# First block of an attention and feed-forward kernel: o in products of 512 tokens, three zero products fewer, and a new order of squares and first weight

## The chip, the cores and the metric

The kernel runs on one core of a Trainium2 chip. The metric is the device time of one execution in microseconds (us). Five runs of the kernel before are known; lower is better. TensorE is called PE here (its weight loads PEld), VectorE DVE, ScalarE ACT, GpSimd POOL, SyncE SP.

## The reference

Two parts follow each other. The first is linear attention over 8 batches, 8 heads, 576 tokens and a head size of 64; the second is a feed-forward layer with a leaky ReLU over 4608 tokens, 512 model columns and 2048 hidden ones.

```python
kv = np.einsum('bhsd,bhse->bhde', k, v)
out = np.einsum('bhsd,bhde->bhse', q, kv)
rms = np.sqrt(np.mean(out * out, axis=-1, keepdims=True) + 1e-06)
attn = (out / rms * g_norm).astype(np.float32)
x = attn.transpose(0, 2, 1, 3).reshape(B * S, H * D)
h = x @ w_in
g = np.maximum(0.01 * h, h)
out = (g @ w_out).astype(np.float32)
```

The two weights arrive as 64-bit floats and are rounded on the chip to 32 bits; all products are of 32-bit floats.

## The kernel before, in words

The tokens are worked off in nine blocks of 512. The blocks after the first save products with Strassen sums; they fill most of the time and are not touched. The change lies in `first_attention`, which makes the first 512 tokens' x before the first block's products can begin, and in `round_f64`, which rounds one weight.

`first_attention` does this. PE warms up on zeros (`keep_warm`, tile `idle_ps`), turns the four q tiles of the first batch (`q_ps`, `rest_ps`; ACT and DVE copy them to `qT`) with one zero product of 256 columns behind each of the first three tiles, makes kv (`kv_ps`, two lots of 36 products, one more zero product between them) and DVE copies it (`copy_kv`). Then come the products of o, 32 of 256 tokens each: tokens 0 to 255 first (`half` 0), then the others, each with the two halves `e` of the head's columns. A product of 32-bit floats shows as two passes in the trace, so 32 products are 64 matmul records and 64 weight loads. The products use different parts of PE's array (64 rows by 32 columns), so that several run at once.

From o the root mean square comes in small steps. ACT squares (`square`), PE adds the squares up per head (`add_up`, tile `sum_ps`), ACT takes the root (`root`, tile `flat`), PE turns it (`turn`), DVE inverts it (`invert`, tile `roots`), PE spreads it (`spread`, tile `inv_ps`), and DVE multiplies x by it (`scale`). x itself is o times the gain `g_sb` (`keep`: DVE for half 0, ACT for half 1).

In between stands the rounding of the first weight (`w0 = rounding(0)`), a generator that `next` moves by a step: ACT's add and cut, then four DVE operations (lines 246, 250, 252, 255). Weights 1 to 4 are rounded behind it (`round_w`), the others within the first block. The products then use the weights in this order, one weight per eight passes of 512 columns: `h_ps` with weight 0, `h_ps` with weight 1, `o_acc` with weight 2, and so on.

Nearly all these instructions are pinned, that is, each engine runs them in the order in which the program lists them. Weight loads are issued by SP in a fixed order, each as soon as its home has been read.

Of the kernel before, what the change touches and what calls it, by code (L numbers as in the profile page):

```python
# [9 lines left out]
F32 = mybir.dt.float32  # L10
U32 = mybir.dt.uint32
I64 = mybir.dt.int64
AF = mybir.ActivationFunctionType
AX = mybir.AxisListType
ALU = mybir.AluOpType
# [8 lines left out]
def kernel(  # L24
# [36 lines left out]
    nc = tc.nc  # L61
    B, H, S, D = q.shape
    DM, DF = w_in.shape
    P = 128
    NE = DM // P
    E = 32
    NP = H // 2
    J = S // 64
    T = S // 32
    NT = 4 * P  # L70
    NB = B * S // NT
    N2 = NT // 2
# [15 lines left out]
    ps_m = ctx.enter_context(tc.tile_pool(name="ps_m", bufs=1, space=bass.MemoryType.PSUM))  # L88
# [28 lines left out]
    def matmul(*args, **kw):  # L117
        pin(nc.tensor.matmul(*args, **kw))  # L118
# [86 lines left out]
    def spare(n, name, dtype=F32):  # L205

        return gpool.tile([P, n], dtype, tag=next(spare_homes), name=name)
# [21 lines left out]
    def round_f64(dst, raw):  # L229

        a, n = dst.shape[1:]
        lo, hi = raw[:, :, 0], raw[:, :, 1]  # L240
        add = spare(a * n, "add", U32)
        pin(nc.scalar.activation(add, lo, func=AF.Copy, scale=2.0 ** -29))
        cut = spare(a * n, "cut")
        pin(nc.scalar.activation(cut, hi.bitcast(F32), func=AF.Copy, scale=2.0 ** -112))
        yield
        pin(nc.vector.tensor_scalar(cut, cut, HIGH_MOST, -HIGH_MOST, op0=ALU.min, op1=ALU.max))
        yield
        dst = dst.bitcast(U32)
        add, cut = (t.rearrange("p (a n) -> p a n", a=a) for t in (add, cut.bitcast(U32)))
        pin(nc.vector.tensor_scalar(dst, cut, 3, None, op0=ALU.logical_shift_left))  # L250
        yield
        pin(nc.vector.scalar_tensor_tensor(dst, in0=cut, scalar=0x80000000, in1=dst,
                                           op0=ALU.bitwise_and, op1=ALU.bitwise_or))
        yield
        pin(nc.vector.tensor_tensor(dst, dst, add, op=ALU.add))  # L255
# [21 lines left out]
    def rounding(j):  # L277
        if w_in.dtype == I64:
            yield from round_f64(w_jobs[j][0], w_raws.pop(j))
# [53 lines left out]
    def o_products(b, lo, hi, e, o_ps):  # L333
        for p in range(NP):
            for l in range(2):
                r = slice(64 * l, 64 * l + 64)
                matmul(o_ps[half_of(p, l)][E * p:E * p + E, :],
                       lhsT=kvs[b % 2][r, p, E * e:E * e + E],
                       rhs=qTs[b][r, p, lo - b * S:hi - b * S], start=True, stop=True)
# [124 lines left out]
    def first_attention():  # L464


        idle = ps_m.tile([P, NT], F32, tag="hd", name="idle_ps")

        def keep_warm(n=NT):
            matmul(idle[:, :n], lhsT=zeros[:, :P], rhs=zeros[:, :n], start=True, stop=True)  # L470

        keep_warm()
        keep_warm()
        qT = qTs[0] = work.tile([P, NP, S], F32, tag="qT", name="qT")
        kv_ps = kv_tiles()


        rest = ps_m.tile([64, NP, P], F32, tag="oc", name="rest_ps")
        for j in range(1, 3):
            load_w(j)  # L480

        def move(p, l, to, of):

            c = 64 * half_of(p, l)
            eng = (nc.scalar.copy, nc.vector.tensor_copy)[l]
            eng(qT[c:c + 64, p, :].rearrange("p (t j) -> p j t", j=J)[:, to, :],
                of[:, :, 64 * l:64 * l + 64])

        for p in range(NP):
            q_in = q_ins.pop((0, p))  # L490
            banks = [ps_m.tile([64, 4, P], F32, tag=t, name="q_ps")
                     for t in (("ha", "hb"), ("hc", "oa"))[p % 2]]
            for j in range(J):
                to = banks[j // 4][:, j % 4, :] if j < 8 else rest[:, p, :]
                pin(nc.tensor.transpose(to, q_in[:, j, :], ident))
            if p + 1 < NP:
                keep_warm(N2)
            for i in range(2):
                for l in range(2):
                    move(p, l, slice(4 * i, 4 * i + 4), banks[i])  # L500
        for p in range(NP):
            for l in range(2):
                move(p, l, slice(8, 9), rest[:, p:p + 1, :])
        for m in range(2):
            if m:
                keep_warm()
            attention_kv(0, m, kv_ps)
        for j in range(3, 7):
            load_w(j)
        w0 = rounding(0)  # L510
        next(w0, None)
        copy_kv(0, kv_ps)
        next(w0, None)


        x = block(0)

        o_ps = [[ps_m.tile([P, 2, N2], F32, tag=t, name="o_ps") for t in tags]
                for tags in (("hb", "hd"), ("oa", "oc"))]
        squares = [[spare(NT, "sq").rearrange("p (e n) -> p e n", e=2) for _ in range(2)]  # L520
                   for _ in range(2)]
        roots = [work.tile([P, 2, 2, NP], F32, tag="rms", name="roots", bufs=2) for _ in range(2)]
        flat = [work.tile([64, N2], F32, tag="t2k", name="flat", bufs=3) for _ in range(2)]
        sum_ps = [ps_att.tile([P, NT], F32, tag="att", name="sum_ps") for _ in range(2)]
        inv_ps = [ps_m.tile([P, 2, N2], F32, tag=t, name="inv_ps") for t in ("ha", "hc")]
        for half in range(2):
            for e in range(2):
                o_products(0, half * N2, half * N2 + N2, e,
                           [o_ps[half][l][:, e, :] for l in range(2)])

        def square(half, l):
            pin(nc.scalar.activation(squares[half][l], o_ps[half][l], func=AF.Square))

        def keep(half, l):
            for e in range(2):
                to, o = x[:, 2 * l + e, half * N2:half * N2 + N2], o_ps[half][l][:, e, :]
                if half == 0:
                    pin(nc.vector.tensor_scalar(to, o, g_sb[:, e:e + 1], None, op0=ALU.mult))
                else:
                    pin(nc.scalar.activation(to, o, func=AF.Copy, scale=g_sb[:, e:e + 1]))  # L540

        def add_up(half, l):

            for e in range(2):
                matmul(sum_ps[half][E * l:E * l + E, :N2], lhsT=group,
                       rhs=squares[half][l][:, e, :], start=(e == 0), stop=(e == 1))

        def root(half):

            pin(nc.scalar.activation(flat[half], sum_ps[half][:64, :N2], func=AF.Sqrt,  # L550
                                     scale=1.0 / D, bias=eps_sb[:64]))

        def turn(half):
            for t in range(2):
                matmul(turned(half)[:, t, :, :], lhsT=flat[half][:, t * P:t * P + P],
                       rhs=ident[:64, :64].rearrange("p (l i) -> p l i", l=2)[:, :, :NP],
                       start=True, stop=True)

        def turned(half):
            return sum_ps[half][:, N2:N2 + 4 * NP].rearrange("p (t l a) -> p t l a", t=2, l=2)  # L560

        def invert(half):
            pin(nc.vector.reciprocal(roots[half], turned(half)))

        def spread(half):

            for l in range(2):
                for t in range(2):
                    for p in range(NP):
                        matmul(inv_ps[half][E * p:E * p + E, l, t * P:t * P + P],  # L570
                               lhsT=roots[half][:, t, l, p:p + 1].to_broadcast([P, E]),
                               rhs=ident, start=True, stop=True)

        def scale(half, l):
            to = x[:, 2 * l:2 * l + 2, half * N2:half * N2 + N2]
            pin(nc.vector.tensor_tensor(
                to, to, inv_ps[half][:, l, :].unsqueeze(1).to_broadcast([P, 2, N2]), op=ALU.mult))

        for l in range(2):
            square(0, l)  # L580
            keep(0, l)
            add_up(0, l)
        next(w0, None)
        square(1, 0)
        add_up(1, 0)
        root(0)
        turn(0)
        next(w0, None)
        invert(0)
        for _ in w0:  # L590
            pass
        square(1, 1)
        add_up(1, 1)
        spread(0)
        root(1)
        turn(1)
        keep(1, 0)
        keep(1, 1)
        scale(0, 0)
        scale(0, 1)  # L600
        invert(1)
        spread(1)
        for l in range(2):
            scale(1, l)
        for j in range(1, 5):
            round_w(j)

# [503 lines left out]
```

## Time and profile before

| what | us |
|---|---|
| median of 5 runs | 929.01 |
| lowest and highest run | 926.81, 929.87 |
| the profiled execution's own time | 928.43 |
| its span, first to last instruction | 926.6 |
| PE busy in the span | 916.2 |
| first `o_ps` matmul | 14.68 |
| first `h_ps` matmul (weight 0) | 28.42 |
| `h_ps` with weight 1 | 32.31 |

The profiled execution lasts 1.83 us longer than its span, and 0.58 us less than the median. A row of the chain of waits gives its start, its length and the work; a row of the timeline gives start, busy time, engine, line, operation and count. "issue" is time for which the profile shows nothing to wait for. In the table of stretches the columns are the stretch, its length, each engine's busy time with the number of instructions, PE's granted clock (1.00 is full), the share of DMA time and GB/s.

### The profile page before, as it was taken

Reading aid. Unit: us, or ns where it says so; the run is one execution under the profiler, and the core shown is the slowest. Engines: PE = TensorE matmul, PEld = TensorE weight load, DVE = VectorE, ACT = ScalarE, POOL = GpSimd, SP = SyncE. Lnnn points to the kernel's source line nnn. Section 1 sums busy time; section 2 is a strip of 40 time slices with the busy share of each in tenths; the row PEclk is TensorE's granted clock in tenths of the full one; section 3 lists DMA queues with packets and bytes.
Section 4 is the critical chain, followed back from the end, with each engine's and each line's share of the span. In section 5 each row is a group of like instructions: output and inputs, shape, how many; then the busy total and the mean of one; then the engine's idle time right before and its main releaser. Section 6 shows DMA issues by size and latency. Waiting matters only on the chain.

```text
span 926.6 us, 17568 instructions
## 1 busy us (share of the span) xinstructions
PE 916.2 (99%) x6856; PEld 776.8 (84%) x6856; DVE 615.9 (66%) x999; ACT 328.9 (35%) x651; POOL 317.5 (34%) x318
## 2 busy tenths in 40 slices
PE   7999999999999999999999999999999999999998
PEld 4544447888998999899999999999989999999997
DVE  4866895587456876587756875687558754654454
ACT  4643632242136232433243423342343333223330
POOL 2000354967722442226211712272225322532222
PEclk9999999999999999999999999999999999999999
DMA  8999916895498679856995589758655676667642
GB/s 251 206 245 242 262 66 202 287 300 166 137 342 268 186 213 308 261 183 181 272 302 180 177 266 284 231 174 247 241 169 182 196 219 185 185 197 220 186 123 91
DMA packets 90081, 200.02 MB, mean 216 GB/s; under 512 B 9872, under 2 KB 42128, under 8 KB 90000
## 3 DMA queue, kind: packets, MB, share of 16 engines
q1 hardware_dynamic: 79536, 186.98, 68.5%
q10 hardware_dynamic: 10016, 10.75, 3.4%
q8 instruction: 54, 0.88, 0.4%
q0 software_dynamic: 448, 1.18, 0.3%
q14 instruction: 27, 0.22, 0.1%
HBM read 172.39 MB, written 26.48 MB: 215 GB/s over the span
## 4 chain that ended last, share of the span: by engine, by line
PE 96%; DVE 2%; DMA 1%; ACT 1%; issue 1%; POOL 0%; DVEq 0%; ACTq 0%; POOLq 0%
PE o_a L118 21%; PE o_c L118 21%; PE h_ha L118 11%; PE h_hb L118 8%; PE h_hc L118 8%; PE h_hd L118 6%; PE o_acc L118 6%; PE h_ps L118 6%; PE o_ps L118 2%; PE kv_ps L118 2%; PE h_a L118 1%; PE h_b L118 1%; PE h_c L118 1%; DMA pairs<-in_v_dram 1%; PE h_d L118 1%
## 5 line engine op out<-in xcount | busy, mean ns | idle before, releaser
L610 POOL TENSOR_TENSOR gs<-g 128x512 f32<-128x512 f32 x64 | 80.8, 1282 | 442.2 <-ACT g L781 440.1
L610 DVE TENSOR_TENSOR o<-o_c,o 128x512 f32<-128x512 f32 (+1 forms) x105 | 71.6, 683 | 117.8 <-PE o_c L118 117.7
L781 ACT ACTIVATE g<-g 128x512 f32<-128x512 f32 x124 | 78.2, 631 | 123.3 <-DVE g L610 123.3
L845 ACT COPY w_all<-h_ha 128x512 f32<-128x512 f32 x84 | 48.7, 580 | 186.6 <-PE h_ha L118 186.6
L610 DVE TENSOR_TENSOR o<-o_a,o 128x512 f32<-128x512 f32 x88 | 60.4, 687 | 63.4 <-PE o_a L118 63.3
L118 PE MATMUL o_c<-pairs,gs 128*128 128x256 f32 x384 | 91.3, 381 | 0.0
L118 PE MATMUL o_a<-pairs,gs 128*128 128x256 f32 x384 | 90.8, 379 | 0.0
L118 PEld LDWEIGHTS o_c<-pairs,gs 128*128 128x128 f32 x384 | 69.8, 190 | 9.3 <-issue 1.4
L118 PEld LDWEIGHTS o_a<-pairs,gs 128*128 128x128 f32 x384 | 69.8, 190 | 7.8
L118 PE MATMUL o_c<-w,g 128*128 128x256 f32 x256 | 61.6, 383 | 0.0
L118 PE MATMUL o_a<-w,g 128*128 128x256 f32 x256 | 61.5, 383 | 0.0
L118 PEld LDWEIGHTS h_ha<-stage,w_all 128*128 128x128 f32 x448 | 58.7, 192 | 2.9
L118 PE MATMUL h_ha<-stage,w_all 128*128 128x128 f32 x448 | 59.0, 275 | 0.0
L118 PE MATMUL h_ps<-xT,w_all 128*128 128x512 f32 (+1 forms) x136 | 57.9, 570 | 0.2 <-DVE w_all L255 0.2
L118 PE MATMUL o_acc<-w,g 128*128 128x512 f32 x128 | 57.8, 595 | 0.0
L610 DVE TENSOR_TENSOR g<-g,pairs 128x512 f32<-128x512 f32 x84 | 55.6, 689 | 1.9
L118 PEld LDWEIGHTS o_a<-w,g 128*128 128x128 f32 x256 | 46.4, 190 | 11.0 <-ACT pairs L845 3.1
L610 POOL TENSOR_TENSOR pairs<-w_all 128x512 f32<-128x512 f32 x8 | 11.1, 1383 | 124.8 <-DMA stage<-in_moe_w_in_dram 96.7
L118 PEld LDWEIGHTS o_c<-w,g 128*128 128x128 f32 x256 | 46.4, 190 | 5.8
L118 PEld LDWEIGHTS h_ps<-xT,w_all 128*128 128x128 f32 x136 | 25.5, 190 | 29.2 <-issue 26.5
L118 PEld LDWEIGHTS o_acc<-w,g 128*128 128x128 f32 x128 | 24.0, 190 | 29.8 <-issue 29.6
L610 DVE TENSOR_TENSOR w_all<-h_hc,w_all 128x512 f32<-128x512 f32 x56 | 38.4, 686 | 15.6 <-PE h_hc L118 15.5
(196 smaller groups left out, 2030.2 us busy)
## 6 DMA issues: line engine op xcount, KB each, us to landing
w_all<-w SPq DMA_DIRECT2D x196, 448.0 KB, 4.1
pairs<-w SPq DMA_DIRECT2D x56, 512.0 KB, 4.5
out_dram<-o ACTq DMA_DIRECT2D x35, 256.0 KB, 4.8
v_in<-in_v_dram SPq DMA_DIRECT2D x29, 288.0 KB, 5.9
k_in<-in_k_dram SPq DMA_DIRECT2D x28, 288.0 KB, 6.3
q_in<-in_q_dram SPq DMA_DIRECT2D x56, 144.0 KB, 6.6
q_in<-in_q_dram SPq DMA_DIRECT2D x56, 140.0 KB, 6.5
w<-stage SPq DMA_DIRECT2D x12, 512.0 KB, 4.7
```

Source lines behind the costliest of these rows:

```text
L118: pin(nc.tensor.matmul(*args, **kw))
L610: ins = eng.tensor_tensor(out_, a, b_, op=ALU.subtract if minus else ALU.add)
L781: nc.scalar.activation(t, t if src is None else src, func=AF.Prelu, alpha=SLOPE)
L845: nc.scalar.copy(q[:, at], banks[tag])
```

## The change

o is now made for all 512 tokens in 16 products, first all of `e` 0, then all of `e` 1, so its tiles hold one `e` each instead of one half each. The three zero products behind the q tiles are gone. The squares of o now all come ahead of the first weight's rounding, which gets one more stopping point; DVE makes x for `e` 0 in two operations of 512, ACT for `e` 1. Sums, roots and turns are made for both halves one after the other, and all four `scale` come last, behind the rest of weight 0. The last lines of `round_f64` and the rounding of weights 1 to 4 are as before.

```diff
         pin(nc.scalar.activation(add, lo, func=AF.Copy, scale=2.0 ** -29))
+        yield
         cut = spare(a * n, "cut")
...
-            if p + 1 < NP:
-                keep_warm(N2)
...
-        w0 = rounding(0)
-        next(w0, None)
         copy_kv(0, kv_ps)
-        next(w0, None)
...
-        o_ps = [[ps_m.tile([P, 2, N2], F32, tag=t, name="o_ps") for t in tags]
+        o_ps = [[ps_m.tile([P, NT], F32, tag=t, name="o_ps") for t in tags]
                 for tags in (("hb", "hd"), ("oa", "oc"))]
...
-        for half in range(2):
+        for e in range(2):
+            o_products(0, 0, NT, e, o_ps[e])
+
+        def add_up(half):
+
+            cols = slice(half * N2, half * N2 + N2)
             for e in range(2):
-                o_products(0, half * N2, half * N2 + N2, e,
-                           [o_ps[half][l][:, e, :] for l in range(2)])
...
+                for l in range(2):
+                    matmul(sum_ps[half][E * l:E * l + E, :N2], lhsT=group,
+                           rhs=squares[e][l][:, cols], start=(e == 0), stop=(e == 1))
...
+        w0 = rounding(0)
+        for e in range(2):
+            for l in range(2):
+                pin(nc.scalar.activation(squares[e][l], o_ps[e][l], func=AF.Square))
+                if e == 0:
+                    pin(nc.vector.tensor_scalar(x[:, 2 * l, :], o_ps[0][l], g_sb[:, 0:1], None,
+                                                op0=ALU.mult))
+        for half in range(2):
+            add_up(half)
+        next(w0, None)
+        next(w0, None)
+        for half in range(2):
+            root(half)
         for l in range(2):
-            square(0, l)
-            keep(0, l)
-            add_up(0, l)
+            pin(nc.scalar.activation(x[:, 2 * l + 1, :], o_ps[1][l], func=AF.Copy,
+                                     scale=g_sb[:, 1:2]))
+        for half in range(2):
+            turn(half)
         next(w0, None)
-        square(1, 0)
-        add_up(1, 0)
-        root(0)
-        turn(0)
         next(w0, None)
         invert(0)
+        spread(0)
+        next(w0, None)
+        invert(1)
+        spread(1)
         for _ in w0:
             pass
-        square(1, 1)
-        add_up(1, 1)
-        spread(0)
-        root(1)
-        turn(1)
-        keep(1, 0)
-        keep(1, 1)
-        scale(0, 0)
-        scale(0, 1)
-        invert(1)
-        spread(1)
-        for l in range(2):
-            scale(1, l)
+        for half in range(2):
+            for l in range(2):
+                scale(half, l)
         for j in range(1, 5):
             round_w(j)
```

## The prediction

> **What bounds the kernel now.** I read the page first, then the chain of waits over the first 40 us, then the timeline and the table of stretches there.
>
> ```profile
> span 926.6 us, 17568 instructions
> PE 916.2 (99%) x6856; PEld 776.8 (84%) x6856; DVE 615.9 (66%) x999; ACT 328.9 (35%) x651; POOL 317.5 (34%) x318
> q8 instruction: 54, 0.88, 0.4%
> ```
>
> PE is busy 99% of the span, so only what lets PE start its long products sooner can help. Queue q8 is PE's own program: 13,712 matmuls and loads come in 54 packets, some 254 instructions each.
>
> ```profile
> 14.68 1.16 PE o_ps L118 x27
> 15.84 2.78 issue
> 18.62 2.78 PE o_ps L118 x37
> 21.40 3.30 PE sum_ps L118 x19
> ...
> 28.63 1.29 DVE xT L576 x2
> 29.92 0.35 DVE cut L246
> ...
> 31.48 0.70 DVE w_all L255
> 32.18 0.14 issue
> 32.31 3.67 PE h_ps L118 x8
> 35.99 3.43 PE o_acc L118 x8
> ```
>
> From 32.31 the chain is PE without a break; before it, it is o, the norm, the last scaling, and the rounding of weight 1. In the middle of o stands a gap of 2.78 us that no semaphore explains. It begins after 27 matmuls and 28 loads of o, 55 instructions.
>
> ```profile
> q8 instruction: 1, 0.02, 5.7%
> ```
>
> That is the DMA view of 15.6 to 17 us: PE's first instruction packet falls there (16,384 bytes from 15.64 to 16.91 us), none in the 15 us before. I read the gap as PE out of instructions.
>
> ```profile
> 14.95:18.36 3.41, 0.89 (x27) 0.42 (x13) 0.07 (x1) 1.20 (x2) 0.00 (x0) 1.00 1.07 235
> 18.36:21.77 3.41, 3.15 (x41) 1.38 (x42) 1.76 (x5) 1.41 (x3) 0.00 (x0) 0.50 1.06 212
> 25.19:28.60 3.41, 2.37 (x56) 1.88 (x47) 1.45 (x3) 3.41 (x9) 0.00 (x0) 1.00 1.13 194
> ```
>
> After a stretch in which PE was busy 26% the clock is at half for 3.41 us; after one at 69% it stays full. So the gap costs twice: 37 passes after it took 2.78 us where 27 ahead of it took 1.16.
>
> **The change part by part.** *Zero products.* Each of the three removed is 2 loads and 2 matmuls, 0.27 us of PE between q tiles. The time is worth nothing: o waits for kv, whose second lot waits for `pairs<-in_v_dram` until 12.68. But the 12 instructions move the packet's edge: 55 + 12 = 67 instructions of o and later lie ahead of it, and o has only 64 now (16 products, two passes, load and matmul; the waits in front of o are the same in number). Margin: 3.
>
> *o.* Ahead of the gap eight passes of 256 columns start every 0.213 us. 32 passes of 512 in eights are 4 x 0.427 = 1.71 us, plus a tail of 0.16: 14.68 to 16.55, `e` 0 ready at 15.70. If they ran at 1.16/27 = 0.043 us per 256 columns it would be 2.75 us; I take 1.71, since the starts are that regular.
>
> *Squares.* Four at a spacing of 0.49 (19.735, 20.229 in the trace): 15.75 to 17.83. They no longer wait behind weight 0, which ACT took at 17.05 when its DMA had landed. Add and cut of weight 0 follow, 1.2 us: 18.95. DVE's two x operations need g_sb, last issued at 5.83 and landed 10.3 us later, 16.2; a 128x512 form isn't in the trace, bounds 0.43 (L246) and 0.78 (two of 256 at 0.39): at most 18.0, and DVE is free until 18.95. Worth nothing.
>
> *The fetch.* PE then has one sum pass left before the edge. Where the packet comes is set by PE's progress or by the DMA queues; PE reaches the edge within 0.5 us of when it did, so I keep 18.62 (bounds: 17.9, when the squares are done; later is the third rival).
>
> *Norm.* Sums: 16 passes, two heads' columns at once, 0.216 apart at full clock: half 0 at 19.65, half 1 at 20.5. Roots (0.47) on ACT 19.7 to 20.15 and 20.55 to 21.0, x of `e` 1 to 22.05. Turns (0.61) end at 20.95 and 21.65. DVE: inverse 21.25, L252 (0.69) 21.95, inverse 22.2, L255 (0.63) 22.85. Spreads (1.08 each, 27.41 to 28.43 before) reach scaling at 22.75 and 23.55. Four scalings, 0.69 at a spacing of 0.61: 22.9 to 25.4. `h_ps` starts at 23.65 and its 3.7 us end at 27.35. Weight 1 follows the scalings on DVE, 2.33 us (29.83 to 32.17 before): 27.75, and PE 0.13 later at 27.9 against 32.31. Gain 4.4 us.
>
> *Clock.* PE now idles 2.0 us from 16.6. With the same stretches it is busy (16.6 - 14.95)/3.41 = 49%, between the 26% that halved the clock and the 69% that didn't. If halved, sums last until 21.9 and the rest moves by 1.65: gain 2.8. The Trainium skill (TensorE: Matmul & The Clock Gate, Part 1: The HAM clock gate) says that the clock falls after at least one idle window of about 3.4 us; by that rule 2.0 us never halves it and the gain is 4.4. The trace contradicts it, 2.78 us were enough, so I take the middle, 0.8 lost: gain 3.6.
>
> A second page speaks against the change. The Trainium skill (Runtime: NRT & Kernel Launch, Instruction fetch mechanics) gives PE 2048 instructions of memory and calls the crossing of a block mostly hidden. Then there would be no stall near instruction 450, fewer instructions would move nothing, and the sum would be the first rival's. The trace shows 2.78 us with the packet in it; I follow the trace.
>
> *Behind it.* Nothing may eat the gain. Weight 2 is ready 1.4 us before PE needs it, weight 3 2.6, from weight 5 on 5 to 12 us (ends of L255 against `o_acc` and `h_ps` starts); DVE's four operations per weight take 2.25 us against PE's 3.43, and they shift with it. What doesn't shift is the DMA: weights 1 to 4 land at 19.5, 21.8, 24.4 and 26.7, and ACT wants them at 21.95, 23.1, 24.3 and 26.75; weight 5 lands at 29.8, wanted at 31.9. SP's issues for weights 8 and 9 (28.05, 29.18) wait for ACT's reads and come earlier. If a weight were 2 us late, PE would lose under 1 us once. PE's later gap (0.4 us at 162.34, behind ACT) follows PE's own products and shifts.
>
> Sum: 928.43 - 3.6 = 924.8 on the profiled execution's scale; the median lies 0.58 above it: 925.4.
>
> **The rivals.** First, that the change doesn't do what it says: PE stops at 15.84 whatever it has left. Then `e` 1 is finished at about 19.6, its squares at 20.85, weight 0's cut at 22.0, roots at 22.9, `h_ps` with weight 1 at about 29.6 to 30.8: gain 1.5 to 2.7, 926.3 to 927.5. For it: the page above. Against it: the packet's place and the count.
>
> Second, a DMA bound: weights 1 to 4 arrive later than before because DMA is already at 1.0 there, and PE waits for them instead. Their rows don't depend on PE, so this needs 2 to 4 us of delay; it would leave a gain of 0 to 2, 927 to 929.
>
> Third, slower: the fetch comes late. It is asked for by PE's progress and shares the DMA engines with the weights; now all sums, not half of o, stand behind it. If it were asked for when PE runs out (about 15.1) and landed like a weight load of SP, 7.3 to 8.5 us later, it would be there at 22.4 to 23.6; the clock would certainly be halved, the path from there to weight 1's product is 9.3 + 1.6 = 10.9 us: 33.3 to 34.5, 1.0 to 2.2 us late, 930.0 to 931.2. It breaks even at 32.31 - 10.9 = 21.4. Against it: the packet's own 1.3 us, and that PE had instructions 1.7 us after it, at 18.62.
>
> **How the numbers follow.** Forecast 0.70 (gain 2.8 to 5.2, the latter with the fetch at 17.9), first rival 0.12, second 0.08, third 0.10. About 0.2%, 1.9 us, is what a measurement here can tell from no change. Faster by more: all of the forecast, most of the first rival, 0.80. Within: the rest of it and the second, 0.10. Slower: 0.10, less certain than the mechanism looks because the fetch's timing is seen once. The range reaches from the best case, 929.0 - 5.2 = 923.8, over both clocks (925.4 ± 0.8) to the first rival's end, 927.5, with 0.4 more at either end for the median of a few runs, which themselves spread over 3 us before.
>
> **What would show it.** Right: 32 `o_ps` matmuls without a gap, ending near 16.6; the gap in `sum_ps`; `h_ps` with weight 1 near 28 to 29.5. The granted clock behind the gap tells 4.4 from 2.8. Wrong: a gap still inside `o_ps`, `sum_ps` resuming after 21.4, or `h_ps` rows that wait for a weight's DMA.

## The result and the profile after

The changed kernel takes 925.74 us (median of 28 runs, 922.83 to 932.86). The kernel before, run beside it, takes 928.44 (47 runs). The ratio is 0.997, 95% interval 0.9959 to 0.998: faster by 2.7 us. The forecast was 925.4. The profiled execution of the changed kernel took 924.76 us, 3.67 less than that of before; its span is 3.6 shorter.

From the page of the changed kernel:

```profile
span 923.0 us, 17491 instructions
PE 913.2 (99%) x6818; PEld 774.7 (84%) x6818; DVE 615.2 (67%) x997; ACT 328.6 (36%) x649; POOL 317.2 (34%) x318
q8 instruction: 54, 0.88, 0.4%
```

The program has 77 instructions fewer, 38 matmuls and 38 loads of PE among them. The chain of waits from 15 us on (start, length, work):

```profile
15.10 2.04 PE o_ps L118 x32
17.15 0.33 PE sum_ps L118
17.48 1.84 issue
19.32 2.46 PE sum_ps L118 x19
...
22.41 1.05 PE inv_ps L118 x32
...
23.55 1.30 DVE xT L560 x2
24.85 0.14 issue
24.98 7.12 PE h_ps L118 x24
32.11 3.43 PE o_acc L118 x8
```

o now runs through: 32 passes in 2.04 us where the kernel before needed 1.16 + 2.78 + 2.78. The gap ("issue", no semaphore behind it) has moved behind o, into the sums, and is 1.84 us long. Counted from the start of the program, PE stops at the same instruction in both kernels. These rows of the table of stretches reach from that start to the stop, first of the kernel before, then of the changed one:

```profile
0.00:15.84 15.84, 13.67 (x219) 9.38 (x220) 6.74 (x19) 6.88 (x14) 5.16 (x14) 1.00 0.79 272
0.00:17.48 17.48, 14.45 (x219) 8.65 (x220) 7.20 (x20) 7.96 (x17) 5.15 (x14) 1.00 0.83 268
```

These are 219 matmuls and 220 loads each time, 1.64 us apart. The packet of PE's program lies from 16.38 to 17.64 us, and PE goes on 1.68 us after its end (before: 16.91 to 18.62, 1.71). The 24 `h_ps` passes hold weight 0 and weight 1; the first with weight 1 starts at 28.51, against 32.31. `o_acc` with weight 2 starts at 32.11 against 35.99. Up to here the change gains 3.8 us.

```profile
16.08:19.49 3.41, 1.57 (x27) 0.43 (x12) 1.41 (x2) 3.09 (x6) 0.00 (x0) 1.00 0.99 233
19.49:22.90 3.41, 3.39 (x43) 2.41 (x43) 1.88 (x6) 2.15 (x6) 0.00 (x0) 1.00 1.12 197
```

The table of stretches shows PE busy 46% around the gap, and a granted clock of 1.00 in the stretch after it. So this execution pays for the gap once, where the profiled execution of before paid twice: part of the 3.67 us between the two is the clock of these two executions.

### The profile page after: what moved, and what is told of

The parts are those of the page before. It is cut to its first block, busy times and chain, and to the rows that moved or that the text cites. A ratio compares the mean times of both kernels' runs of the same rounds, so it can differ in the third digit from the quotient of the medians.

```text
span 923.0 us, 17491 instructions
## 1 busy us (share of the span) xinstructions
PE 913.2 (99%) x6818; PEld 774.7 (84%) x6818; DVE 615.2 (67%) x997; ACT 328.6 (36%) x649; POOL 317.2 (34%) x318
## 4 chain that ended last, share of the span: by engine, by line
PE 96%; DVE 1%; DMA 1%; issue 0%; POOL 0%; ACT 0%; DVEq 0%; POOLq 0%
PE o_a L118 21%; PE o_c L118 21%; PE h_ha L118 11%; PE h_hb L118 8%; PE h_hc L118 8%; PE h_hd L118 6%; PE o_acc L118 6%; PE h_ps L118 6%; PE o_ps L118 2%; PE kv_ps L118 2%; PE h_a L118 1%; PE h_b L118 1%; DMA pairs<-in_v_dram 1%; PE h_c L118 1%; PE h_d L118 1%; DVE g L598 0%
## 5 line engine op out<-in xcount | busy, mean ns | idle before, releaser
L598 DVE TENSOR_TENSOR w_all<-h_hc,w_all 128x512 f32<-128x512 f32 x56 | 38.4, 686 | 15.6 <-PE h_hc L118 15.5
```

What stands on the lines that cost most here:

```text
L598: ins = eng.tensor_tensor(out_, a, b_, op=ALU.subtract if minus else ALU.add)
```

## The experiments

My theory: PE stops after a fixed number of instructions until its program's next packet is there. The change moves o to the near side of that edge by two edits that are each too small alone. The rivals: the stop is fixed in time; the gain is the new order of squares and weight; the packet is asked for only when PE gets to the edge. Below, "at full clock" means runs with a mean granted clock of 0.9985 or more; one half-clock stretch of 3.41 us in 925 lowers the mean to 0.998. The medians are of 6 to 22 runs each; the kernel before has 146 runs beside all of these, median 928.38, 79 of them at full clock with 927.45, 67 below with 929.14.

**Each half of the change alone.** First, the changed kernel with the three zero products put back:

```diff
+            if p + 1 < NP:
+                keep_warm(N2)
```

> The changed kernel with the three zero products between the q tiles put back, so that the packet's edge lies after 55 instructions of o again. Theory A (PE runs out of instructions at a place set by their count): the gap opens after 27 or 28 of the 32 passes of o; e 1 is finished only behind the gap, near 19.5 us, its squares at 20.6, the first root at 21.8 instead of 20.4; 1.4 to 2.2 us over the changed kernel, so a gain of 0.5 to 1.5 us over the kernel before. Theory B (the gap comes at a time, not at a count, and the gain is that of the new order alone): within 0.4 us of the changed kernel, a gain near 2.7.

926.6 us, ratio 0.9988 (0.9978 to 0.9998). The chain of waits:

```profile
15.79 2.02 PE o_ps L118 x27
17.80 1.02 issue
18.83 1.08 PE o_ps L118 x5
```

With 12 instructions more in front of it the gap stands inside o again, after the same 27 passes as before. Second, the kernel before without the zero products (the same two lines taken out of it):

> The kernel before with nothing changed but the three zero products left out. Theory A: the gap moves from behind 27 passes of o to behind 33 of 64, so half 0 of o is complete ahead of it; but its squares still stand behind weight 0 on ACT (18.3 us), so they move up by 1.4 us and the end of o by 0.5: a gain of 0.5 to 1.5 us. Theory B: the gap stays where it is in time, at the same pass give or take two, and nothing is gained (0 +- 0.3).

928.41 us, ratio 1.0003 (0.9988 to 1.0018): no gain, where 0.5 to 1.5 us were expected. Eleven of its 14 runs are below full clock.

```profile
14.56 1.24 PE o_ps L118 x33
15.80 2.86 issue
18.66 1.09 PE o_ps L118 x31
```

The gap comes 6 passes, 12 instructions, later: 33 instead of 27. Third, the changed kernel with o in 32 products of 256 tokens:

```diff
-            o_products(0, 0, NT, e, o_ps[e])
+            for half in range(2):
+                cols = slice(half * N2, half * N2 + N2)
+                o_products(0, half * N2, half * N2 + N2, e, [o[:, cols] for o in o_ps[e]])
```

> The changed kernel with o in 32 products of 256 tokens, in the new order of e: 128 instructions, 67 of them ahead of the edge. The theory: the gap opens after 33 of 64 passes, e 1 is made behind it, near 20 us; its squares end at 21 instead of 18.5, 1.5 to 2.5 us over the changed kernel, so little of the gain is left (927 to 928). If the new order alone made the gain: within 0.4 us of the changed kernel.

926.99 us, ratio 0.9982 (0.9973 to 0.9991).

```profile
14.41 1.24 PE o_ps L118 x33
15.65 2.37 issue
18.02 1.51 PE o_ps L118 x31
```

The same 33 passes. In all these kernels PE stops after 219 matmuls and 220 loads, wherever in o or the sums that falls and whether it is at 15.65 or at 17.80 us: a count, not a time. Both edits are needed to bring o in front of the edge. They are not needed for all of the gain: at full clock this kernel takes 925.62 (7 runs) and the one with its zeros back 926.08 (14 runs), against 924.71 of the changed kernel and 927.45 of before. So the new order without o's escape brings 1.4 to 1.8 us of the 2.7, and the escape the last 0.9 to 1.4. Which part of the new order brings its share was not isolated.

**The edge moved on purpose.** In the changed kernel one zero product at the start becomes 25 small ones, 96 instructions more:

```diff
-        keep_warm()
+        for _ in range(25):
+            matmul(idle[:32, :32], lhsT=zeros[:, :32], rhs=zeros[:, :32], start=True, stop=True)
```

> The changed kernel with its second zero product of 512 columns at the start replaced by 25 zero products of 32 columns: 96 more instructions, so that the edge lies 29 instructions before o, in the second lot of kv. Asked for at the edge (theory A1): the packet starts 0.7 to 1.5 us after PE's sequencer gets there, 14 to 15 us, PE goes on about 3 us after it stopped, near 17; o ends near 19.2, 2 us over the changed kernel. Asked for one packet earlier and held back by the loads (A2): 96 instructions earlier is in the q tiles, 1 to 2 us earlier than before, but the packet still comes when the first batch's loads have drained, at 15.6 to 16.4, and PE goes on at 17.3 to 18.1: 2.3 to 3 us over. If the request is early and not held back, the packet comes at 10 to 13 us and there is no gap at all: a gain of up to 2 us over the changed kernel.

929.69 us, ratio 1.0013 (1.0003 to 1.0024).

```profile
12.88 1.17 PE kv_ps L118 x58
14.05 2.94 issue
16.99 0.76 PE kv_ps L118 x14
```

The gap now lies in kv's second lot, 14 passes from its end. That is what the count says: 67 instructions lay ahead of the edge from o on, 96 - 67 = 29 of kv are pushed behind it, and 14 passes are 28. The stop is 2.94 us long, the clock is at half for two stretches (15.43 to 22.26), and all of the gain is gone. A fetch in this place costs 4 to 5 us on this path, half clock included. The packet began at 14.63, and PE went on at 16.99: these are the times expected if the packet is asked for at the edge (14 to 15, near 17), not those for a request one packet earlier (15.6 to 16.4, 17.3 to 18.1). The run with a late o, below, says the opposite.

**Squares or first weight first.** The changed kernel with the add and cut of weight 0 on ACT ahead of the squares:

```diff
         w0 = rounding(0)
+        next(w0, None)
+        next(w0, None)
         for e in range(2):
...
-        next(w0, None)
-        next(w0, None)
         for half in range(2):
             root(half)
```

> The changed kernel with the add and cut of weight 0 back in front of the squares on ACT. Theory A: the squares start when weight 0 has landed and been read, at 18.3 to 19.5 instead of 16.4 us, and end at 20.4 to 21.5; the sums follow them, not the fetch; weight 1's product 0.7 to 2 us later than in the changed kernel. Rival: the fetch and the clock set the time of the sums anyway: within 0.3 us.

924.84 us, ratio 0.9959 (0.9944 to 0.9975); at full clock 924.73 against 924.71. The order of squares and weight is worth nothing that these runs can show, as long as the fetch's gap is there.

```profile
16.75 0.66 ACT add L242
17.41 0.55 ACT cut L245
17.96 0.49 ACT sq L568
18.45 0.04 issue
18.50 3.48 PE sum_ps L118 x20
```

All four squares come behind the weight here, and PE goes on at 18.50, right behind the first of them: the wait (16.87 to 18.50) is now for the squares. The packet ended at 16.99, and by the 1.4 to 1.7 us of the other profiles PE would have had its instructions at 18.4 to 18.7 anyway. `h_ps` with weight 1 starts at 28.71, 0.2 us later than in the changed kernel.

**When is the packet asked for?** The copies of kv are made six times, so that o starts 1.4 us later than in the changed kernel:

```diff
-        copy_kv(0, kv_ps)
+        for _ in range(6):
+            for i in range(2):
+                pin(nc.vector.tensor_copy(kvs[0][:, i::2, :], kv_ps[i]))
```

> The changed kernel with DVE's two copies of kv done six times over, so that o starts 2.5 us later with not one instruction more or less on PE. If the packet is asked for when PE reaches the edge (A1), the gap stays: it opens 2.5 us later and PE goes on 2.9 to 3.0 us after the edge's instructions are handed out, near 21.8; weight 1's product 2.5 us later than in the changed kernel, 928.2. If it is asked for a packet's length earlier and held back by the loads (A2), it comes at 15.6 to 16.4 as before, PE has its instructions near 19, o ends at 19.6 and there is no gap; the sums wait for the squares (20.9) instead, 1.0 to 1.8 us over the changed kernel.

926.31 us, ratio 0.9976 (0.9968 to 0.9984). The chain of waits, then the DMA view of 15.1 to 16.45 us:

```profile
14.06 2.26 DVE kv L511 x11
16.32 0.14 issue
16.46 3.76 PE o_ps L118 x32
20.22 3.70 PE sum_ps L118 x20
```

```profile
q8 instruction: 1, 0.02, 5.9%
```

The packet ran from 15.16 to 16.44, while PE still waited in front of o, 67 instructions short of the edge, and there is no gap. So the packet was asked for before PE's array came to the edge. These rows show when the array works, not how far PE's sequencer has read ahead of it; had it read 67 instructions ahead, the request could still be one made at the edge. The later packets speak against that. In the changed kernel the third one begins at 38.91, and up to there PE has done this:

```profile
0.00:38.91 38.91, 33.32 (x347) 20.05 (x348) 25.29 (x55) 21.55 (x40) 5.15 (x14) 1.00 0.97 246
```

These are 695 instructions; in the 14 profiles it is 675 to 727. The first edge lies at 439, and a packet brings about 250, so PE has just used up the first packet and has the second still ahead of it. This fits a request one packet ahead. By the same count the first packet would be asked for near instruction 190, which PE passes at 10.2 to 12.4 us. Its start lies between 14.63 and 16.38 us, 3.4 to 5.5 us later, and with the edge moved it comes about as late (4.4 us) as elsewhere. That is inferred from counts; no run tests it. What holds the packet back was not isolated: DMA is busy when it comes (1.10 from 15 to 16 us in the profile of before), but from 12 to 14 us its share is below 0.4.

The kernel with the late o lost its own 1.4 us and the clock (half from 15.59 to 22.42, o in 3.76 us), and still is 2.1 us faster than the kernel before.

**Filling the gap, and fewer zeros.** One of the zero products at the start is moved behind o, where PE has nothing else to do:

```diff
-        keep_warm()
         keep_warm()
...
             o_products(0, 0, NT, e, o_ps[e])
+        matmul(inv_ps[1].rearrange("p a n -> p (a n)"), lhsT=zeros[:, :P], rhs=zeros, start=True, stop=True)
```

> The changed kernel with one of the two zero products of the start moved behind o; the count ahead of the edge is the same, less 4 at the front and 4 more at the back, and the first sum instruction falls behind the edge. PE is busy 0.86 us longer into the gap, which shrinks from 1.84 to about 1.0 us. If the clock's half stretches come from this gap, fewer runs than three in ten show a clock under 0.9985 and the median falls by 0.3 to 0.9 us; runs at full clock stay the same. If they come from elsewhere (the start, which is now colder, or later waits), the share stays or rises.

924.07 us in six runs, all at full clock, ratio 0.9949 (0.9929 to 0.9969). That would be a gain over the changed kernel. The same kernel measured once more, and the changed kernel beside it:

> The kernel with one zero product of the start moved behind o, once more, on the same chip as the changed kernel. If filling the gap is what counts: 923.5 to 924.6, over 1 us under the changed kernel, and nearly every run at a granted clock of 0.9985 or more. If six runs were luck: the changed kernel's 925.7 and its three runs in ten at a lower clock.

> The changed kernel itself, beside the two others of this call: 925 to 926, three runs in ten at a granted clock under 0.9985, and these 2 to 3 us longer than the rest.

925.15 (12 runs, 3 below full clock) and 925.35 (12 runs, 4 below); ratios 0.9975 (0.9959 to 0.9991) and 0.9983 (0.9963 to 1.0002). At full clock 924.69 and 924.61. The move is worth nothing that these runs can show; the six first runs were a lucky draw. The gap was 0.17 us in the first profile of the moved product, 0.98 in the second, and 1.29 in that of the changed kernel's copy; they ended at 18.33, 18.94 and 18.14. The fetch alone differs by that much from one execution to the next. The changed kernel without the zero product between the two lots of kv:

```diff
-            if m:
-                keep_warm()
```

> The changed kernel without the zero product between the two lots of kv as well: 4 instructions fewer, so that 7 of the sums lie ahead of the edge, and PE idle for 1.6 us ahead of kv's second lot instead of 0.8. If idle PE time near the edge is what halves the clock: more than half of the runs under 0.9985, median 926.5 to 928, though runs at full clock are as fast as the changed kernel's (924.7). If the zero product does nothing for the clock: 925 to 926.

924.04 us (8 runs), ratio 0.9958 (0.9945 to 0.9972); at full clock 923.82. Had PE's idle time near the edge been what halves the clock, more than half of the runs would have been below full clock; one of eight was. The kernel may be 0.8 us better than the changed one, but the intervals overlap. Then sums of 512 columns, all three remaining zero products left out, and the roots ahead of weight 0's add and cut on ACT:

```diff
-        keep_warm()
-        keep_warm()
...
-            if m:
-                keep_warm()
...
-                    matmul(sum_ps[half][E * l:E * l + E, :N2], lhsT=group,
-                           rhs=squares[e][l][:, cols], start=(e == 0), stop=(e == 1))
+                    matmul(sum_ps[0][E * l:E * l + E, :], lhsT=group,
+                           rhs=squares[e][l], start=(e == 0), stop=(e == 1))
...
+        add_up()
         for half in range(2):
-            add_up(half)
+            root(half)
         next(w0, None)
         next(w0, None)
-        for half in range(2):
-            root(half)
```

> The changed kernel with sums of 512 tokens (16 instructions instead of 32), the roots ahead of weight 0 on ACT, and all six zero products gone, so that 15 of the 16 sum instructions lie ahead of the edge. The theory: only the last pass waits for the fetch; sums end at 19.9 instead of 21.1, roots at 20.9 instead of 21.7, and weight 1's product comes 0.7 to 1.2 us earlier than in the changed kernel, 924.5 to 925.0. Rival: the zero products hold the clock; without them q and kv run at half clock, o begins later or runs at half clock, and more runs than the changed kernel's three in ten have a granted clock under 0.9985: 926 to 928.

927.17 us, ratio 0.9986 (0.9976 to 0.9996); 21 of 22 runs below full clock. The gap in front of the sums was gone, but the PE groups of 12 to 26 us show what came instead:

```profile
L118 PE MATMUL inv_ps<-ident,roots 128*32 128x128 f32 x64 | 3.4, 396 | 1.5 <-DVE roots L542 1.5
...
L118 PE MATMUL sum_ps<-ident,flat 64*128 64x8 f32 x8 | 1.1, 255 | 0.6 <-ACT flat L529 0.6
```

PE waits 0.6 us for the roots and 1.5 for the inverses, and the clock goes to half from 22.57 to 25.98. Weight 0 stands ahead of the inverses:

```profile
20.52 0.56 ACT cut L245
...
21.10 0.44 DVE cut L247
...
21.56 0.43 DVE w_all L251
21.99 0.17 DVE roots L542
```

DVE inverts behind two of its operations on weight 0, and these wait for ACT's cut. ACT began weight 0 at 19.87 instead of 18.32, because this edit puts it behind the roots; in this profile a weight's load landed late as well (19.75). So the longer wait is at least in part the edit's own, and what wide sums alone would bring is not shown. The rival, that q and kv run at half clock without the zero products, is half right: the first stretch of full clock begins at 8.91 us, and eight passes of the q turns ahead of it took 1.89 us, where they take 1.04 behind it. But o began at 14.57 at full clock, no later than in the changed kernel (15.10).

**A second place that can halve the clock.** A run below full clock costs the kernel before 1.7 us (929.14 against 927.45), half of 3.41. In the changed kernel 12 of 40 runs are below, and they take 3.0 us more (927.74 against 924.71): more than one half-clock stretch can cost. In four of the twelve the mean clock is 0.996 or less, which takes two stretches; the other eight still have a median of 927.9. Three profiles show where such an execution loses more: those of the kernel with its zeros back, of the one without the middle zero product, and of the one with wide sums. The chain of waits of the first of them:

```profile
84.13 8.12 DMA v_in<-in_v_dram
92.25 0.14 issue
92.39 1.76 PE kv_ps L118 x70
```

In its table of stretches:

```profile
89.55:92.96 3.41, 1.62 (x41) 0.79 (x43) 0.82 (x2) 2.58 (x5) 0.00 (x0) 1.00 0.89 199
92.96:96.37 3.41, 3.41 (x50) 2.17 (x41) 3.24 (x7) 2.52 (x5) 0.00 (x0) 0.50 0.93 264
```

The kv products of the second batch wait for its last v. In the profile of before this load landed at 90.61 and PE wanted it at 92.84; in that of the changed kernel at 88.51, wanted at 88.96. The slack was 2.23 us there and is 0.45 here. The need moved up by 3.9 us with the change; the landing differs by more from one profile to the next (85.5 us in the kernel before without its zero products, 92.25 at the latest) than between these two. In the three profiles it landed at 92.25, 90.88 and 92.25, and PE stood still for 1.8 to 2.5 us. In the first two a stretch of half clock follows. In the third, with wide sums, the clock stays full:

```profile
87.42:90.83 3.41, 2.72 (x8) 0.95 (x6) 0.00 (x0) 0.91 (x2) 0.00 (x0) 1.00 1.03 207
90.83:94.24 3.41, 1.85 (x72) 1.58 (x73) 2.49 (x5) 3.41 (x7) 0.00 (x0) 1.00 0.96 209
```

The stop of 2.25 us lies across the border of two stretches, and PE is busy for over half of each. The last experiment took the wait away, by loading k and v of that batch's last two pairs ahead of their q:

```diff
-                        load_pair(*nxt)
+                        load_pair(*nxt, "kv")
+                for nxt in () if apart else pairs_next:
+                    load_pair(*nxt, "q")
```

> The changed kernel, but the k and v of the second batch's last two pairs are loaded ahead of the q of these pairs. Theory: the runs of the changed kernel at a lowered clock come from the second batch's kv products, which wait at about 89 us for a v load that lands between 85.5 and 92.3 us. Here that load is issued some 5 us earlier (at about 75 instead of 80 us) and lands at about 82 to 86, so PE has no gap at 88 to 92, the runs at a lowered clock fall below 3 in 10, and the median is 924.5 to 925 (that of the runs at full clock stays at 924.6). Rival: the lowered clock comes from the gap at the instruction fetch at about 17 us; then the share of runs at a lowered clock stays at about 3 in 10 and the median at 925.5. A second rival: the q loads are late instead and the turns of q make PE wait, over 926.5.

932.24 us, ratio 1.0043 (1.0027 to 1.0059), slower than both kernels. The v now lands at 82.18 and PE has no gap at kv, so that part worked. But PE waits for DVE further on, at 130.2 for 2.27 us and at 137.9 for 2.63, each followed by half clock:

```profile
129.92:133.33 3.41, 1.14 (x3) 0.49 (x3) 3.41 (x5) 1.10 (x3) 2.64 (x2) 1.00 0.00 0
133.34:136.75 3.41, 3.41 (x5) 1.35 (x4) 3.41 (x4) 0.00 (x0) 3.33 (x5) 0.50 0.34 115
136.75:140.16 3.41, 1.12 (x3) 0.19 (x1) 3.41 (x4) 0.60 (x1) 3.41 (x4) 1.00 0.00 0
140.16:143.57 3.41, 3.07 (x4) 1.51 (x5) 3.21 (x6) 0.00 (x0) 2.59 (x3) 0.50 0.00 0
```

DVE is busy all the time there (3.41 of 3.41), with POOL beside it: DVE's cut (L247) takes 1.4 us each from 132.3 to 135.2, mostly 0.42 elsewhere. The edit touches loads alone, but the order that DVE and ACT work in isn't the changed kernel's from 99 us on: the weight that DVE begins at 103.5 in the changed kernel it begins at 107.4 here, and POOL's sums start at 130.6 instead of 121.5. Two waits and twice half of 3.41 make 8.3 us, near the 7.5 lost against 924.7. The range of one rival (over 926.5) holds, but not its reason: PE waited for weights, not for a turn of q. Why the order changes was not found, and all six runs are below full clock. None of the expectations described this, and the question for which the run was made stays open: whether the changed kernel's runs below full clock come from the v load or from the fetch. For the v load speak the size (3.0 us, and 4.3 in the two sets of 12 runs) and that two of the three profiles with a late v lost the clock there; no profile of the changed kernel itself was such a run.

## Why the prediction was right

**The mechanism: right.** The edge is a count, the 12 instructions and the halved number of o passes move o to its near side, and the margin was 3: in the profile exactly two loads and one matmul of the sums run between o and the gap. The first rival (a fixed time) falls with the 27, 33 and 33 passes and with the shift by 96 instructions. Its price was right all the same: it gave a gain of 1.5 to 2.7 with a stop inside o, and the two kernels of the new order that stop there gain 1.5 and 1.6 on the runs of before beside them (1.4 and 1.8 at full clock). My 254 instructions per packet divided by all of PE's program; the first 439 come without one of these packets, so about 246 is the better figure. The third rival's price was seen only where the edge was moved on purpose (929.69), not by the fetch's timing: PE went on at 19.32, well ahead of the break-even of 21.4. That the packet can come while PE still stands in front of o (o started late) also weakens the ground of that rival, a request when PE runs out.

**The path: each term close, with one common shift.** o began 0.42 us later than in the profile of before (15.10; its v landed at 13.10 instead of 12.68), and took 2.04 instead of 1.87. The fetch, kept at 18.62, came at 19.32. The sums and turns behind it took 3.09 us, worked out as 3.03. `h_ps` started at 24.98 against 23.65: 0.7 of the shift, and another 0.65 because both scalings of half 0 are done before it, where I let it start behind the first. That was harmless, since 3.53 us of weight 0 and weight 1's own rounding (ready 28.28, worked out 27.75) end nearly together. Weight 1's product: 28.51, worked out 27.9.

**The size: right by errors that partly cancel.** I took the middle between a gain of 4.4 at full clock and 2.8 at half. The profiled executions differ by 3.67 without a halved clock after; the missing 0.7 is the later fetch (0.6 of it at weight 1's product). The step that was wrong is the one that put the clock's risk on the changed kernel alone. Nearly half the runs of before (67 of 146) are below full clock and its profiled execution was one of them; between runs at full clock the gain is 927.45 - 924.71 = 2.7 us, not 4.4. The changed kernel is below full clock less often (12 of 40, which may be chance), but such runs cost 3.0 us there, not 1.7; over all runs the two nearly cancel, and the gain is again 2.7. The half clock in the profile of before was thus counted as a loss of every run, 1.7 us too much, and the 0.8 set against it for the changed kernel's clock made up for half of that. The time came out closer than the gain (3.6 forecast, 2.7 measured) by luck: the five runs of before lay at 929.01, 0.6 above the 928.44 of the 47.

**"Nothing may eat the gain": wrong in part.** I checked weights 1 to 9 against PE and left out the k and v loads of the next batch. One of them had a slack of 2.23 us in the profile of before, smaller than the gain. In the first block itself the step held: no `h_ps` or `o_acc` row up to 60 us waits for a weight.

**The rule on the clock.** The Trainium skill's rule (TensorE: Matmul & The Clock Gate, Part 1: The HAM clock gate; an idle window of about 3.4 us) gives a gain of 4.4. The profile after did keep its clock, but a PE idle for part of such a window was enough in the profile of before, and my middle between the two had no measured ground. What the traces show is in the last section.

## What to carry to other kernels

When an instruction stall stands at a fixed count, count instructions and decide what shall lie in front of it; but look at what PE would do in the gap, for work that waits for other engines there (roots, inverses) may hide behind it. A profiled execution has its own state of the clock: before taking a stretch of half clock as gain, ask in how many runs of the kernel before it appears. A gain at the front of a chain is taken from the slack of every load further on that doesn't move with it: list landing against need for those too.

## What had not been expected of the hardware

The clock changes in windows of 3.41 us that lie on a grid, and the grid's place differs from one execution to the next. In the records every full-clock stretch before the end is a whole number of windows: in the profile of before 4 windows, one at half, then 265. The first of these stretches began between 4.7 and 8.9 us in the profiles. Whether a gap halves the clock seems therefore to depend on how it falls on the grid. The kernel before without its zero products has a longer gap (2.86 us) than the kernel before (2.78), and its profiled execution kept the clock, where a border cut the gap in two:

```profile
13.58:16.99 3.41, 1.75 (x66) 1.26 (x59) 0.57 (x3) 0.71 (x2) 0.00 (x0) 1.00 1.01 261
16.99:20.40 3.41, 1.74 (x39) 0.91 (x38) 2.79 (x7) 2.02 (x4) 0.00 (x0) 1.00 1.05 234
```

Nine windows with PE busy 0.89 to 1.62 us (26 to 47%) were followed by half clock; those with 1.74 or more (51%) were not. Three others below half kept the clock: 1.57 us in the changed kernel, and 1.41 and 1.45 in the last windows with PE work of two profiles (loads of k and v first, late o). So the border near half is not exact in these terms. Coming back takes more: in the kernel with late o a window at half clock with 2.55 us busy was followed by another at half, one with 3.07 by full clock elsewhere. My stretch from 14.95 to 18.36 for the changed kernel (its 49% is 48 by the numbers given) was laid on the grid of another execution.
